# A third expert's tokens turned by DMA instead of TensorE, and two router counts handed out one slot later

## The chip, the cores and the metric

The kernel runs on one core of a Trainium2 chip. The metric is the device time of one execution in microseconds (us), as a median of several runs; a lower time is better. Engines are named as the profile does: PE is TensorE (PEld its weight loads), DVE is VectorE, ACT is ScalarE, POOL is GpSimd, SP is the engine that issues most DMAs.

## The reference, cut to what matters

A windowed attention over 8 batches and 8 heads gives 4608 tokens of 512 values. A mixture of 8 experts follows. Every expert takes exactly 576 tokens, given out greedily in the order of the largest logits:

```python
cap = N // E                       # 4608 // 8 = 576
logits = x @ w_gate
order = np.argsort(-logits.flatten())
for idx in order:                  # the best free (token, expert) pair first
    tok, e = int(idx) // E, int(idx) % E
    if assigned[tok] >= 0 or counts[e] >= cap:
        continue
    assigned[tok] = e
    counts[e] += 1
for e in range(E):
    mask = assigned == e
    out[mask] = np.maximum(x[mask] @ w1[e], 0.0) @ w2[e]
```

## The kernel before

The attention runs first and writes its tokens `x` to device memory. The experts follow from about 230 us on. In what order the experts are done is decided on the chip: the *router* finds, in phases 0 to 7, the expert that is full next and the list of its 576 tokens. Below, "expert k" is the k-th that is worked on (k = 0 to 7), and phase k of the router gives its number (`r.ei[k]`) and its token list (`r.idx[k]`).

**An expert** has two layers. `layer1` (lines 1077 to 1107) makes 8 blocks f of 128 hidden values for 576 tokens, cut in two halves of 288. Each value is held as a high and a low part in a reduced float32 format (`xh` and `xl` for tokens, two planes of a weight tile), and three products are added, so a block has 24 matmuls, the layer 192. ACT evicts a result with Relu (line 1100), and DVE makes its low part (line 1105); four PSUM banks serve for this. `layer2` (lines 1109 to 1137) makes five output tiles t of 128 tokens (the last one of 64) from 24, the last one 16, matmuls, 112 in all, in two PSUM banks; ACT evicts (line 1130), and POOL scatters the rows to the output (line 1135).

**Weights** come in chunks: SP loads one (line 994), ACT casts the high part (line 1001), DVE subtracts for the low part (line 1003, two per chunk).

**Tokens** of expert k + 1 are brought while expert k is worked on. POOL gathers five tiles of token rows by an indirect DMA (line 1012). They must be turned, so that the 512 values lie along the partitions. There are two ways:

- `turn` (lines 1023 to 1042): per tile four transposes on PE (line 1036), ACT rounds the result into `xh` (line 1039), DVE subtracts for `xl` (line 1040).
- `turn_by_dma` (lines 1047 to 1075): per tile two copies on ACT split the 32-bit words into two planes of 16 bits (line 1056), SP issues a transposing DMA (line 1061), two copies on ACT put the words together again (line 1071), ACT rounds into `xh` (line 1073), DVE subtracts for `xl` (line 1074).

`BY_DMA = 2` says that the second way is taken while experts 2 to 6 are worked on, so for the tokens of experts 3 to 7. The tokens of experts 0, 1 and 2 go the first way.

**Slots.** `layer1` yields 16 times and `layer2` 15 times; at each yield `slot(k, i)` (lines 1219 to 1256) hands out side work, with i from 0 to 30. In layer 1 a slot is 12 matmuls long. In layer 2 a tile has three slots, of 9, 9 and 6 matmuls (of 6, 6 and 4 in the last tile). Due slots are written in tables: `W_LOAD` and `W_SPLIT` for the weights of this and the next expert, `DMA_AT[k]` for the 16 steps of `turn_by_dma` (gather, five pairs of plane copies, five transposes, five times word copies with rounding and subtraction). The first way starts at slot 16 with the gather, three slots later with the first tile, and goes on with every second slot.

The router's phases are one generator. What it yields is the number of slots until it goes on: in `few` (lines 886 to 936) a phase makes a comparison of candidates on DVE (`ind`, line 617), yields `WAITS[2]` = 3 slots plus `FAR` = 2 in the first of three steps of phases 1 to 3, and then counts with eight small matmuls on PE (line 641). One slot after that comes a sum over the partitions (line 661), three slots later the next count; after the third step follow line 796 (one slot), lines 822 and 823 (three slots) and the token list from line 853 (four slots). A phase may go on only while the list for expert k + 1 or k + 2 is still missing.

**What sets the order on an engine.** A slot says when an instruction is handed out, and so its rank. A builder then fills each engine's queue before the run: it works with estimated durations, takes the ready instruction of the highest rank, and can put work earlier or later than its slot. On the chip each queue runs in that order, and a waiting instruction holds up what stands behind it. `behind` (line 1044) keeps plane and word copies behind the last eviction that was handed out before them. `xh` and `xl` have one buffer each, the ring `g` of token tiles and planes has seven.

Of the kernel before, what the change touches and what calls it, by code (L numbers as in the profile page):

```python
# [445 lines left out]
WAITS = (2, 1, 3, 1, 1, 3, 3)  # L446
TURN_WAIT, TURN_STEP = (6, 3), (1, 2)
TURN0 = 3
BY_DMA = 2
DMA_AT = {2: [10, 11, 11, 12, 12, 12, 13, 13, 13, 13, 13, 23, 24, 25, 26, 27], 3: [0, 4, 5, 6, 7, 8, 9, 9, 9, 9, 9, 18, 20, 22, 24, 26]}  # L450
BEHIND = mybir.DependencyInfo(mybir.DependencyClass.NoSync, mybir.DependencyReason.SCHED_ONLY)
BIG = 1e30
MAGIC = 12582912.0
# [1 line left out]
CUTS = 2  # L455
STEPS = 3
FEW = 16
FAR = 2
FIRST = 27
EARLY_CUTS = 3  # L460
EXACT_STEPS = 12
# [3 lines left out]
def bc(ap, shape):  # L465
    return ap.to_broadcast(shape)
# [17 lines left out]
class Router:  # L484
# [401 lines left out]
    def few(self, k, b, am, sel):  # L886


        nc, rt = self.nc, self.p["rt"]
        lo, w, rw = yield from self.ends(b, False)  # L890
        q, t = self.small("q", NT), self.small("qt", NT)
        nc.vector.tensor_scalar(w, w, 1.0 / J ** 2, None, ALU.mult)
        nc.vector.tensor_scalar(rw, rw, float(J ** 2), None, ALU.mult)
        half = self.small("half")
        nc.vector.scalar_tensor_tensor(half, w, 0.5, lo, ALU.mult, ALU.add)
        nc.vector.tensor_scalar(q, b, self.hi[:, 0:1], half[:, 0:1], ALU.min, ALU.max)
        nc.vector.tensor_scalar(q, q, half[:, 0:1], rw[:, 0:1], ALU.subtract, ALU.mult)
        nc.vector.tensor_scalar(q, q, MAGIC, MAGIC, ALU.add, ALU.subtract)
        nc.vector.scalar_tensor_tensor(t, q, 8.0, am, ALU.mult, ALU.add)
        nc.vector.scalar_tensor_tensor(t, b, BIG, t, ALU.is_lt, ALU.mult)  # L900
        c = self.small("few", FEW)
        for i in range(0, FEW, 8):
            nc.vector.max(c[:, i:i + 8], t)
            if i + 8 < FEW:
                nc.vector.match_replace(t, c[:, i:i + 8], t, 0.0)
        f, y = self.small("fq", FEW), self.small("fy", FEW)
        nc.vector.tensor_scalar(y, c, 0.125, -0.5625, ALU.mult, ALU.add)
        nc.vector.tensor_scalar(f, y, MAGIC, MAGIC, ALU.add, ALU.subtract)
        fa = rt.tile([128, FEW], BF, name="fa")
        nc.vector.scalar_tensor_tensor(fa, f, -8.0, c, ALU.mult, ALU.add)  # L910
        OH = rt.tile([128, 8, FEW], BF, name="OHf")
        nc.vector.tensor_tensor(OH, self.C["eb"][:, :, 0:FEW], bc(fa.unsqueeze(1), [128, 8, FEW]), ALU.is_equal)
        base = None
        for s in range(STEPS):
            step = float(J ** (2 - s))
            if s == 0:
                nc.vector.tensor_scalar(y, f, 1.0 / step, -0.5 + 0.5 / step, ALU.mult, ALU.add)
            else:
                nc.vector.tensor_scalar(y, f, base[:, 0:1], 1.0 / step, ALU.subtract, ALU.mult)
                nc.vector.tensor_scalar(y, y, float(J), -0.5 + 0.5 / step, ALU.min, ALU.add)  # L920
            key = rt.tile([128, FEW, 2], BF, name="kf")
            nc.vector.tensor_scalar(key, bc(y.unsqueeze(2), [128, FEW, 2]), MAGIC, MAGIC, ALU.add, ALU.subtract)
            ind = rt.tile([128, NT, J], BF, name="ind", bufs=1)
            self.indicate(ind, key, 0, FEW)
            yield WAITS[2] + (s == 0 and k < 4) * FAR
            cnt = self.count(ind, OH, 0, FEW)
            n = yield from self.enough(cnt, self.base)
            low = self.small("lq")
            if s == 0:
                nc.vector.memset(low, -step)  # L930
            else:
                nc.vector.tensor_scalar(low, base, -step, None, ALU.add)
            base = self.small("bq")
            nc.vector.scalar_tensor_tensor(base, n[:, 0:1], step, low, ALU.mult, ALU.add)
        nc.vector.tensor_scalar(sel, q, base[:, 0:1], None, ALU.is_ge)
        nc.vector.scalar_tensor_tensor(self.hi, base, w[:, 0:1], lo, ALU.mult, ALU.add)
# [252 lines left out]
def layer_moe(tc, P, C, r, x, w1, w2, out, exact):  # L1189
# [29 lines left out]
    def slot(k, i):  # L1219
# [18 lines left out]
        for e, layer, c, due in W_SPLIT:  # L1238
            e += k
            if i >= due and len(W.get((e, layer), (0,) * 9)) == c and len(raws[e, layer]) > c:  # L1240
                W[e, layer].append(m.split(raws[e, layer][c]))
                break
        if k >= BY_DMA and k + 1 in r.idx:
            if k not in gathers:
                asked[k + 1] = []
                gathers[k], st["made"] = m.turn_by_dma(r.idx[k + 1], asked[k + 1]), 0
            due = DMA_AT[min(k, 3)]
            while st["made"] < len(due) and i >= due[st["made"]]:
# [108 lines left out]
```

## Time and profile before

| | us |
|---|---|
| median of 3 runs | 678.37 (676.81 to 679.53) |
| the profiled execution, its own time | 674.45 |
| its span, first to last instruction | 672.7 |
| TensorE busy in it | 646.4 |
| VectorE busy | 471.6 |
| ScalarE busy | 384.0 |
| expert 1, layer 2 (from 319.07) | 30.37 |
| expert 2, layer 1 (from 349.44) | 28.81 |
| expert 2, layer 2 (from 378.25) | 27.07 |

The page gives busy times of the engines and shares of the chain that ended last. The views in order of time give the start of each instruction in us from the start of the span, its duration, and in brackets the idle time of its engine before it with what ended it. Neighbours of one kind are merged (x2 and so on). The time of a stretch is read from starts: a matmul's end is modelled, and one begins before the one ahead of it has ended.

### The profile page before, as it was taken

How to read it: one execution, taken by the hardware profiler on the slowest of the kernel's cores; microseconds unless marked ns; L12 is line 12 of the kernel's file. 1: busy time of each engine (PE TensorE's matmuls, PEld its weight loads, DVE VectorE, ACT ScalarE, POOL GpSimd, SP SyncE). 2: the span in 40 equal slices, each digit the busy share in tenths (PEclk: the TensorE clock that was granted, in tenths of full speed). 3: DMA queues.
4: the chain of work that ended last, by engine and by line, in shares of the span. 5: the costliest groups of instructions: out<-in, count | busy, mean ns of one | idle time of the engine just before them, and what ended most of it. 6: DMA issues, size and time to landing. Idle time of an engine off the chain costs nothing.

```text
span 672.7 us, 18974 instructions
## 1 busy us (share of the span) xinstructions
PE 646.4 (96%) x7152; PEld 573.0 (85%) x7152; DVE 471.6 (70%) x1985; ACT 384.0 (57%) x1096; POOL 136.2 (20%) x296
## 2 busy tenths in 40 slices
PE   8999999999995799999999999999999999999996
PEld 5999998888984498889779879989989989988985
DVE  6898888888986899879669788866756625423310
ACT  7998988789973253334234566465545555654200
POOL 4121122122120301511423123023014014011011
PEclk9999999999997799999999999999999999999999
DMA  8656756556521543615406637527536556421001
GB/s 291 191 188 198 222 183 204 185 167 208 163 78 54 155 166 118 235 40 188 165 34 236 171 103 240 118 106 219 117 111 213 132 119 201 128 71 40 1 25 51
DMA packets 58980, 98.13 MB, mean 146 GB/s; under 512 B 27648, under 2 KB 37120, under 8 KB 58880
## 3 DMA queue, kind: packets, MB, share of 16 engines
q1 hardware_dynamic: 52992, 77.96, 38.5%
q0 software_dynamic: 5888, 18.88, 8.5%
q8 instruction: 58, 0.95, 0.6%
q14 instruction: 42, 0.34, 0.2%
HBM read 72.04 MB, written 18.87 MB: 135 GB/s over the span
## 4 chain that ended last, share of the span: by engine, by line
PE 78%; DVE 13%; DMA 3%; ACT 2%; issue 2%; POOL 0%; SPq 0%; POOLq 0%; DVEq 0%; ACTq 0%
PE ph L1095 22%; PE po L1123 9%; PE po L1124 9%; PE s L66 7%; PE po L1126 7%; PE pt L66 7%; PE pt L178 6%; PE x L66 6%; DVE hl L1003 3%; DMA raw<-in_w_dram 2%; DVE hlo L1105 2%; ACT u L159 2%; PE m L641 1%; DMA g<-x,idx 1%; PE pg L1036 1%
## 5 line engine op out<-in xcount | busy, mean ns | idle before, releaser
L1095 PE MATMUL ph<-xh,hl 128*128 128x288 f32 (+2 forms) x1024 | 188.5, 298 | 0.4 <-DVE hlo L1105 0.3
L1095 PEld LDWEIGHTS ph<-xh,hl 128*128 128x128 f32 x1024 | 154.7, 189 | 2.0 <-issue 0.8
L1123 PE MATMUL po<-hl,hh 128*128 128x512 f32 (+1 forms) x328 | 128.4, 391 | 0.0
L159 ACT ACTIVATE u<-u,mn 128x192 f32<-128x192 f32 (+2 forms) x288 | 125.4, 439 | 2.9 <-DVE mn L149 2.9
L1124 PE MATMUL po<-hl,hh 128*128 128x512 f32 (+1 forms) x328 | 126.3, 385 | 0.0
L1095 PE MATMUL ph<-xl,hl 128*128 128x288 f32 (+2 forms) x512 | 115.6, 297 | 0.0
L1100 ACT ACTIVATE hh<-ph 128x288 fp32r<-128x288 f32 (+2 forms) x128 | 46.6, 408 | 106.4 <-PE ph L1095 103.4
L1126 PE MATMUL po<-hl,hlo 128*128 128x512 f32 (+1 forms) x264 | 101.3, 384 | 0.0
L1003 DVE TENSOR_TENSOR hl<-raw,hl 128x512 fp32r<-128x512 f32 x128 | 85.2, 684 | 22.8 <-ACT hl L1001 22.6
L149 DVE CUSTOM_DVE_ANT_0 u<-s,bm 128x192 f32<-128x192 f32 (+2 forms) x308 | 91.9, 333 | 8.1 <-PE s L66 4.5
L1135 POOL DMA_INDIRECT out_dram<-o,idx x40 | 41.8, 1045 | 273.6 <-ACT o L1130 206.4
L1095 PEld LDWEIGHTS ph<-xl,hl 128*128 128x128 f32 x512 | 84.2, 189 | 0.2 <-DVE xl L1074 0.2
L1001 ACT CAST hl<-raw 128x1024 fp32r<-128x1024 f32 x64 | 65.8, 1050 | 23.9 <-DMA raw<-in_w_dram 21.4
L1105 DVE SCALAR_TENSOR_TENSOR hlo<-ph,hh 128x288 fp32r<-128x288 f32 (+2 forms) x128 | 49.2, 416 | 32.2 <-ACT hh L1100 31.5
L1123 PEld LDWEIGHTS po<-hl,hh 128*128 128x128 f32 x328 | 61.8, 188 | 11.2
L1124 PEld LDWEIGHTS po<-hl,hh 128*128 128x128 f32 x328 | 61.7, 188 | 11.2
L1130 ACT COPY o<-po 128x512 f32<-128x512 f32 (+1 forms) x33 | 18.9, 574 | 90.1 <-PE po L1126 79.9
L66 PE MATMUL s<-qk 64*64 64x192 f32 (+1 forms) x1112 | 62.4, 320 | 2.2 <-issue 1.1
L178 PE MATMUL pt<-ident_sb,u 128*128 128x128 f32 x368 | 57.7, 278 | 0.7 <-ACT u L159 0.6
L1126 PEld LDWEIGHTS po<-hl,hlo 128*128 128x128 f32 x264 | 49.6, 188 | 9.9
L1012 POOL DMA_INDIRECT g<-x,idx x40 | 43.0, 1075 | 64.9 <-DMA raw<-in_w_dram 26.5
L159 ACT ACTIVATION_READ_ACCUMULATOR u<-u,mn 128x1 f32 x288 | 55.2, 192 | 0.0
(249 smaller groups left out, 921.2 us busy)
## 6 DMA issues: line engine op xcount, KB each, us to landing
raw<-in_w_dram SPq DMA_DIRECT2D x64, 512.0 KB, 4.4
qk<-in_qk_dram SPq DMA_DIRECT2D x32, 576.0 KB, 4.5
v<-in_v_dram SPq DMA_DIRECT2D x32, 288.0 KB, 3.0
x<-xb SPq DMA_DIRECT2D x14, 512.0 KB, 3.5
x<-xb SPq DMA_DIRECT2D x8, 128.0 KB, 3.3
x<-xb SPq DMA_DIRECT2D x4, 256.0 KB, 2.2
g<-x,idx POOLq DMA_INDIRECT x40, 4.2
out_dram<-o,idx POOLq DMA_INDIRECT x40, 2.8
```

Of the source, the lines that this page charges most:

```text
L66: put(nc.tensor.matmul(out, w, a, start=start, stop=stop, skip_group_check=True))
L149: put(nc.vector.tensor_tensor_reduce(out=u[rows], in0=x[rows, c:c + 64 * m].rearrange("q (j k) -> q j k", k=64), in1=bm[n % NP][rows, y:y ...
L159: put(nc.scalar.activation(u, u, AF.Exp, bias=st["mn"][:, i:i + 1], scale=-1.0, accum_out=st["sm"][:, i:i + 1]))
L178: put(nc.tensor.transpose(ps[:, c:c + 128], u[:, o + 128 * j:o + 128 * j + 128], ident))
L1001: self.last = nc.scalar.copy(hl[:, 0, :], raw)
L1003: nc.vector.tensor_tensor(hl[:, 1, c:c + 512], raw[:, c:c + 512], hl[:, 0, c:c + 512].bitcast(F32), ALU.subtract)
L1095: nc.tensor.matmul(pp[t], w[:, a, j, fo:fo + 128], x[:, j, cut[t]:cut[t + 1]], start=(i == 0), stop=(i == 11))
L1100: self.acted = nc.scalar.activation(o, pp[t], AF.Relu)
L1105: nc.vector.scalar_tensor_tensor(d, pp[t][:, c0:c1], 0.0, o[:, c0:c1].bitcast(F32), ALU.max, ALU.subtract)
L1123: nc.tensor.matmul(out, a, wh, start=(f == 0), stop=False)
L1124: nc.tensor.matmul(out, a, wl, start=False, stop=(f == 7 and t == 4))
L1126: nc.tensor.matmul(out, hl[:, f, 128 * t:128 * t + 128], wh, start=False, stop=(f == 7))
```

## The change

Two things change. `BY_DMA` becomes 1, so the tokens of expert 2 are turned in the second way, while expert 1 is worked on. A row of due slots is added for it: the gather at slot 14, the plane copies at 15 and 16, the transposes at 17, word copies, roundings and subtractions at 23 to 27. And `FAR` becomes a table by phase: it stays 2 for phases 1 and 2, becomes 3 for phase 3 (it was 2) and 1 for phase 4 (it was 0).

```diff
-BY_DMA = 2
-DMA_AT = {2: [10, 11, 11, 12, 12, 12, 13, 13, 13, 13, 13, 23, 24, 25, 26, 27], 3: [0, 4, 5, 6, 7, 8, 9, 9, 9, 9, 9, 18, 20, 22, 24, 26]}
+BY_DMA = 1
+DMA_AT = {1: [14, 15, 15, 16, 16, 16, 17, 17, 17, 17, 17, 23, 24, 25, 26, 27], 2: [10, 11, 11, 12, 12, 12, 13, 13, 13, 13, 13, 23, 24, 25, 26, 27], 3: [0, 4, 5, 6, 7, 8, 9, 9, 9, 9, 9, 18, 20, 22, 24, 26]}
...
-FAR = 2
+FAR = (0, 2, 2, 3, 1, 0, 0, 0)
...
-            yield WAITS[2] + (s == 0 and k < 4) * FAR
+            yield WAITS[2] + (FAR[k] if s == 0 else 0)
```

## Rows read from the trace of the kernel before

**Rows 1.** The page: busy time, share of the span and instructions of each engine; the chain that ended last by engine.

```profile
PE 646.4 (96%) x7152; PEld 573.0 (85%) x7152; DVE 471.6 (70%) x1985; ACT 384.0 (57%) x1096; POOL 136.2 (20%) x296
...
PE 78%; DVE 13%; DMA 3%; ACT 2%; issue 2%; POOL 0%; SPq 0%; POOLq 0%; DVEq 0%; ACTq 0%
```

**Rows 2.** Busy time by engine in three layers: expert 1's layer 2, expert 2's layer 1 and layer 2 (stretch, its length, then busy us and instructions of PE, PEld, DVE, ACT and POOL, the granted clock of TensorE as a share of full speed, the DMA share and GB/s); and the one line of a late layer 1 from the chain in order of time (start, length, matmuls).

```profile
319.07:349.44 30.37, 29.54 (x162) 23.25 (x161) 18.14 (x69) 8.71 (x14) 10.31 (x9) 1.00 0.31 109
349.44:378.25 28.81, 27.71 (x230) 26.77 (x229) 27.12 (x108) 14.64 (x29) 7.47 (x8) 1.00 0.61 199
378.25:405.32 27.07, 27.07 (x146) 21.37 (x144) 21.75 (x98) 14.38 (x25) 4.69 (x5) 1.00 0.43 116
...
564.34 25.58 PE ph L1095 x192
```

**Rows 3.** The transposes in expert 1's layer 2: the line's matmuls in that stretch, then TensorE in order of time at the second and at the last of the five groups.

```profile
L1036 PE MATMUL pg<-ident_sb,g x20: 222/272/307, 327.8 to 345.2; 128*128 128x128 f32 x16, 64*128 64x64 f32 x4
...
331.87 0.60 PE L1036 MATMUL pg<-ident_sb,g 128*128 128x128 f32 x4
332.22 0.47 PE L1123 MATMUL po<-hl,hh 128*128 128x512 f32 x1
332.54 0.39 PE L1124 MATMUL po<-hl,hh 128*128 128x512 f32 x1
...
344.97 0.46 PE L1036 MATMUL pg<-ident_sb,g 64*128 64x64 f32 x4
345.36 0.50 PE L1123 MATMUL po<-hl,hh 128*128 128x512 f32 x1
```

**Rows 4.** TensorE in order of time around the first count of phase 3, and VectorE's comparison for that count.

```profile
326.12 0.39 PE L1124 MATMUL po<-hl,hh 128*128 128x512 f32 x1
326.35 0.39 PE L1126 MATMUL po<-hl,hlo 128*128 128x512 f32 x1
327.56 0.42 PE L641 MATMUL m<-OHf,ind 128*128 128x16 bf16 x8 [0.83 <-DVE ind L617]
...
326.81 0.69 DVE L617 TENSOR_TENSOR ind<-kf,c_i 128x1024 bf16<-128x1024 bf16 x1
```

**Rows 5.** TensorE around the first count of phase 4 in expert 2's layer 1, VectorE's comparison for it, the matmuls of layer 1 alone up to phase 3's token list (line 853) and up to that count (stretch, length, PE busy and matmuls, PEld), and the engines' busy time from phase 3's last sum to the comparison's end.

```profile
372.85 0.69 PE L1095 MATMUL ph<-xh,hl 128*128 128x288 f32 x4
374.37 0.42 PE L641 MATMUL m<-OHf,ind 128*128 128x16 bf16 x8 [0.83 <-DVE ind L617]
...
373.62 0.69 DVE L617 TENSOR_TENSOR ind<-kf,c_i 128x1024 bf16<-128x1024 bf16 x1
...
349.44:359.55 10.11, 9.78 (x72) 9.53 (x71) 1.00 0.56 197
349.44:374.36 24.92, 23.46 (x170) 22.63 (x169) 1.00 0.64 215
...
347.09:374.32 27.23, 26.18 (x201) 24.93 (x200) 26.61 (x101) 12.85 (x24) 8.19 (x9) 1.00 0.61 206
```

**Rows 6.** The way by DMA as it runs for expert 3's tokens: groups of instructions with their busy time and mean ns (plane copies over the whole span, word copies and roundings in expert 2's layer 2), the five issues on SP, and the end of it in order of time on ScalarE, VectorE and TensorE.

```profile
L1056 ACT COPY pl<-g 128x512 uint16<-128x512 uint16 x40 | 22.2, 627 | 1.1 <-DMA g<-x,idx 1.1
...
L1071 ACT COPY xf<-tp 128x512 uint16<-128x512 uint16 x8 | 5.6, 778 | 0.0
...
L1073 ACT CAST xh<-xf 128x512 fp32r<-128x512 f32 x4 | 2.5, 620 | 0.1
...
L1061 SPq DMA_TRANSPOSE tp<-pl x5: 1231/1261/1358, 376.1 to 382.9; - x5
...
403.19 0.41 ACT L1073 CAST xh<-xf 128x256 fp32r<-128x256 f32 x1
403.50 2.00 ACT L1001 CAST hl<-raw 128x1024 fp32r<-128x1024 f32 x2
...
405.36 0.42 DVE L1074 TENSOR_TENSOR xl<-xf,xh 128x256 fp32r<-128x256 f32 x1
...
405.58 0.66 PE L1095 MATMUL ph<-xl,hl 128*128 128x288 f32 x2
406.08 0.29 PE L1095 MATMUL ph<-xh,hl 128*128 128x288 f32 x1
```

**Rows 7.** Around the gather for expert 2: VectorE's token list, GpSimd's first and last gather with the time from issue to landing, the weight loads on SP, the eviction of layer 2's first tile and the late weight casts on ScalarE; and from the page the low halves of the weights.

```profile
316.72 0.33 DVE L861 SCALAR_TENSOR_TENSOR idx<-ia 64x5 int32<-64x5 f32 x2
...
317.83 1.22 POOL L1012 DMA_INDIRECT g<-x,idx  x1 [12.54 <-issue]
...
323.40 2.52 POOL L1012 DMA_INDIRECT g<-x,idx  x1 [0.30 <-issue]
...
DMA to landing us min/median/max: 3.5/5.5/6.5
...
319.81 1.66 SPq L994 DMA_DIRECT2D raw<-in_w_dram  x2
...
324.78 0.59 ACT L1130 COPY o<-po 128x512 f32<-128x512 f32 x1 [4.00 <-PE po L1126]
...
346.59 2.11 ACT L1001 CAST hl<-raw 128x1024 fp32r<-128x1024 f32 x2 [0.75 <-PE po L1124]
...
L1003 DVE TENSOR_TENSOR hl<-raw,hl 128x512 fp32r<-128x512 f32 x128 | 85.2, 684 | 22.8 <-ACT hl L1001 22.6
```

## The prediction

> **What bounds the kernel now.** I read the first two parts of the page, then the busy time by layer of the experts, then the instructions in order of time around each place that the diff touches. TensorE is busy 96% of the span and carries 78% of the chain that ended last [rows 1]; its granted clock is 1.00, the higher of its two levels (2.4 GHz), in the layers in question [rows 2]. So a microsecond is won only where TensorE issues less or waits less. In the experts it hardly waits at all: PE is idle for 0.83 us in expert 1's layer 2, for 1.10 us in expert 2's layer 1, and not at all in expert 2's layer 2 [rows 2]. The two layers with waits are the ones that the diff touches. Layer 2 of expert 1 (30.37 us) also carries the transposes of expert 2's tokens; layer 2 of expert 2 (27.07 us), beside which the next tokens go by DMA, does not.
>
> A busy share hides part of a wait, since the end of a matmul is modelled. I therefore count from start to start: a layer 2 matmul starts every 0.23 us [rows 4], a layer 1 matmul every 0.133 us (a late layer, without router work, has 192 in 25.58 us, [rows 2]).
>
> **Part 1: expert 2's transposes leave TensorE.** Twenty transposes in five groups of four stood in expert 1's layer 2 [rows 3]. A group that follows the router's count costs 0.39 us up to the next matmul (344.97 to 345.36); there are three such. A group alone costs 0.35 us (331.87 to 332.22), and the matmul behind it lasts 0.32 instead of 0.23 us until the next start, which makes 0.44 us; there are two. Sum: 3 x 0.39 + 2 x 0.44 = 2.05 us, all of it on the bounding engine. The count's own switch stays.
>
> **Part 2: what replaces them.** Ten plane copies on ScalarE of 0.63 us each, ten word copies (eight of 0.78, the two short ones taken no dearer), five roundings of 0.62 [rows 6]: at most 6.3 + 7.8 + 3.1 = 17.2 us, less the five evictions that go. ScalarE is busy only 8.71 of 30.37 us in that layer [rows 2], so the sum fits. VectorE's five subtractions change their input, not their number. The gather is handed out at slot 14 instead of 16, but that moves nothing: GpSimd starts it at 317.83, right after the index is written at 316.72 + 0.33 [rows 7]. SP gets five transposes of about 1.3 us [rows 6]. The loads that could queue behind them, two chunks of expert 2's first weights, are issued from 319.81 on, before any plane can exist (first landing 317.83 + 3.5 = 321.3), and their casts start at 346.59 [rows 7]: 25 us of cover, so nothing.
>
> What isn't hidden is the end. The last part of the tokens goes word copy, rounding, subtraction, and layer 1 begins at once. For expert 3, which already goes this way, the last rounding ran 403.19 to 403.60 and its subtraction 405.36 to 405.78, while layer 1 asks for it at 405.58; the two matmuls from there take 0.50 us to the next, where 2 x 0.133 are due, a loss of about 0.25 us [rows 6]. Expert 2's will follow the same slots 23 to 27. Bounds: 0, not below, since expert 2's layer 1 starts without such a gap now, and the 4.8 us of the last rival below; I take 0.25, from the nearest row.
>
> Taken by itself the new way is the slower one: four transposes pass TensorE in 0.35 to 0.39 us [rows 3], one transposing DMA keeps SP for about 1.3 us [rows 6]. I go by who is the bound: TensorE is, SP isn't. A rule of the Trainium skill speaks against this part: "VectorE: DVE Perf Modes", The three transpose paths and Rules for kernel authors, gives a 128x128 transpose (of 16-bit values) 390 ns on TensorE and 1309 ns by the DMA crossbar, and advises TensorE wherever a PSUM destination will do. The trace agrees on the order of the two; by the rule the time would rise, and the last rival works out by rows what that would be, 680.4.
>
> **Part 3: phase 3's first count one slot later.** In expert 1's layer 2 the matmul after 326.35 was due at 326.58 and started at 327.56: 0.98 us of wait for the comparison that VectorE ran 326.81 to 327.50 [rows 4]. It stood at its due slot 19: 326.58 is 7.51 us, or some 33 matmuls of 0.23, behind the layer's start, the 24 of the first tile and nine of the second. Slot 20 lies nine matmuls, 9 x 0.23 = 2.07 us, further, more than the 0.98 that is missing, and the comparison does not wait for the count, so it would be 1.1 us early. Gain 0.98 us; bounds 0 and 0.98.
>
> **Part 4: phase 4's first count.** The same wait stands in expert 2's layer 1: due at 372.85 + 4 x 0.133 = 373.38, started at 374.37, 0.99 us, behind the comparison at 373.62 [rows 5]. But here the due time isn't what places it. Phase 3's last step stood after 72 matmuls, slot 5; two slots and three later is slot 10, 132 matmuls; the count stands after 170 [rows 5]. The built order has already put it back to where the comparison was thought ready, and VectorE is busy 26.61 of the 27.23 us up to there [rows 5]. Phase 3's extra slot makes phase 4's due slot 12 (6 + 2 + 4), 156 matmuls, still ahead of 170. So the extra slot of phase 4 need not bind, and VectorE's chain, which starts about a slot later as well, sets the time. Bounds: 0.99 gained, and 1.6 lost if the whole slot (12 x 0.133) shows; I take 0, since the row that decides is VectorE's busy one.
>
> The rest of phases 3 and 4 moves by one and two slots. Expert 3's gather waits for phase 3's index, so its planes come up to 1.6 us later; between the planes' transposes (slot 13) and their use (slot 23) lie ten slots, which hide it. If that cover were gone, TensorE would pay it one to one. Phase 5 is held back until expert 3 in both, so nothing moves behind it.
>
> **Sum.** -2.05 - 0.98 + 0.25 = -2.78 us. The profiled execution took 674.45 us, 672.7 of span and 1.75 around it; 671.7 would be its time afterwards. The median of the runs shown lies 3.92 us above that execution, at 678.37; the saving is a count of matmuls and waits and doesn't scale with that, so 675.6.
>
> **Rivals.**
> A second wait that goes too: the slot binds after all, or VectorE's order changes in favour. -2.78 - 0.99 = -3.77, 674.6. For it: the first wait has the same size and cause. Against it: 170 against 132.
>
> ScalarE's queue blocked: the plane copies wait for the gather, and the eviction of layer 2's first tile (324.78) stands behind them. The last gather is issued at 323.40 and lands at most 6.5 us after its issue [rows 7], 329.9; two copies and the eviction (0.59) end near 331.7. The third tile, which needs the bank, would start near 332.22 - 0.98 - 0.39 - 0.35 = 330.5. Loss up to 1.2, so 676.8. For it: one gather wait of 1.1 us stands before the plane copies already [rows 6]. Against it: in order of readiness the eviction comes first.
>
> The other side, late tokens: the two weight casts that become possible at 346.59 (2.11 us, [rows 7]) go ahead of the last word copies on ScalarE, and their four low halves (4 x 0.68, [rows 7]) ahead of the last subtraction on VectorE. For expert 3 the casts came behind the last rounding, but directly, at 403.50 [rows 6]. Layer 1 of expert 2 then starts 2.1 + 2.7 = 4.8 us late: -2.78 + 4.8 = +2.0, 680.4. It decides against the change from a lateness of 2.8 us on top of the 0.25. This is what the transpose rule quoted above would amount to: a longer path that nothing hides any more.
>
> **How the numbers follow.** Chances: forecast 0.42, second wait gone too 0.25, blocked eviction 0.18, late tokens 0.15. The range goes from the second case less the 1.2 us by which the runs shown spread, 673.4, to the last case, 680.4. About 0.5% (3.4 us) is what a measurement of this kernel can tell from no change: below 675.0 or above 681.8. The forecast lies 0.6 us inside "same", so with a spread of 1.2 to 1.6 us it gives about 0.13 to faster, the second case 0.16, the third 0.02: 0.31. Slower gets part of the last case and a little for what isn't listed, 0.10; the rest, 0.59, is same.
>
> **What would show it.** Right: no transposes of line 1036 in layer 2 of expert 1, that layer near 27.3 us; no wait of TensorE for the comparison in it; a wait of about 1 us still in layer 1 of expert 2; two or three stretched starts when that layer begins. Wrong: a gap ahead of layer 2's third tile (blocked eviction), a gap of over 1 us at expert 2's first matmuls (late tokens), a count in expert 2 that starts without a wait, or new gaps in experts 2 and 3 from planes that come late.

## The result, and the profile after

The changed kernel takes 680.75 us (median of 20 runs, 677.71 to 684.99), the kernel before 677.49 (20 runs, 675.34 to 680.05): a ratio of 1.0053 with a 95% interval of 1.0037 to 1.0068, by the ratio some 3.6 us slower. The forecast was 2.8 us faster, 675.6, and the dearest of its rivals 680.4. The profiled execution took 681.35 us, 679.6 of it span. That of before was faster than each of the 20, so two more profiles of the kernel before and one more of the changed kernel were taken. Lengths from start to start, in us:

| stretch | before, three profiles | after, two profiles |
|---|---|---|
| time of the execution | 674.45, 679.38, 680.10 | 681.35, 683.15 |
| expert 1, layer 2 | 30.37, 30.46, 30.44 | 33.75, 34.17 |
| expert 2, layer 1 | 28.81, 30.97, 29.84 | 28.48, 29.58 |
| expert 2, layer 2 | 27.07, 27.06, 27.04 | 28.81, 29.60 |
| expert 3, layer 1 | 27.60, 28.61, 28.88 | 28.88, 28.74 |

The loss is in expert 1's layer 2, where the gain had been forecast: 3.5 us, by the means of the profiles. Expert 2's layer 2 adds 2.2; the two layers 1 differ about as much between executions of one kernel.

The page, busy time by engine (answers to [rows 1]): TensorE has its twenty instructions less, ScalarE its twenty more.

```profile
PE 645.5 (95%) x7132; PEld 572.5 (84%) x7132; DVE 470.6 (69%) x1985; ACT 395.6 (58%) x1116; POOL 135.7 (20%) x296
```

Busy time in three layers (answers to [rows 2], same columns), then in two stretches of the first of them.

```profile
318.07:351.82 33.75, 29.32 (x142) 23.00 (x140) 17.12 (x66) 19.58 (x34) 8.17 (x8) 0.90 0.49 134
351.82:380.30 28.48, 27.54 (x224) 26.60 (x223) 26.93 (x109) 12.73 (x25) 8.65 (x9) 1.00 0.61 195
380.30:409.11 28.81, 27.53 (x153) 21.53 (x152) 20.09 (x83) 16.79 (x30) 4.99 (x4) 1.00 0.42 109
...
329.13:333.99 4.86, 0.43 (x3) 0.05 (x2) 1.77 (x6) 3.33 (x6) 1.01 (x1) 0.78 0.63 128
333.99:338.40 4.41, 4.41 (x11) 3.45 (x12) 1.48 (x6) 0.11 (x1) 0.98 (x1) 0.50 0.94 187
```

PE is idle for 4.4 of 33.75 us where it was idle for 0.83, and the granted clock is 0.90 where it was 1.00. Both come from one place. TensorE in order of time around phase 3's first count (answers to [rows 4]):

```profile
327.39 0.39 PE L1126 MATMUL po<-hl,hlo 128*128 128x512 f32 x1
327.62 0.42 PE L641 MATMUL m<-OHf,ind 128*128 128x16 bf16 x8
...
329.12 0.40 PE L1126 MATMUL po<-hl,hlo 128*128 128x512 f32 x1
333.94 0.19 PE L661 MATMUL m<-sat,c_ones 128*128 128x1 bf16 x1 [4.43 <-DVE sat L658]
333.99 0.78 PE L1123 MATMUL po<-hl,hh 128*128 128x512 f32 x1
334.56 0.63 PE L1124 MATMUL po<-hl,hh 128*128 128x512 f32 x1
334.99 0.63 PE L1126 MATMUL po<-hl,hlo 128*128 128x512 f32 x1
```

The count itself (327.62) starts without a wait, as forecast. Behind a count VectorE works out the router's answer to it (lines 649 to 658), and a sum on TensorE takes that answer. This sum starts 4.82 us after the matmul ahead of it, where 0.23 are due: 4.6 lost. Behind it eleven matmuls take 4.41 us instead of 11 x 0.23 = 2.5, at a granted clock of 0.50 (the 1.2 GHz level): 1.9 more. Who was late is to be read in the chain that ended last, in order of time (start, length, what):

```profile
321.14 7.03 DMA g<-x,idx
328.19 0.28 ACT pl L1056
...
328.90 1.65 ACT pl L1056 x3
330.55 0.48 ACT o L1130
331.03 0.95 ACT hl L1001
332.01 1.29 DVE hl L1003 x2
...
333.74 0.16 DVE sat L658
333.94 0.19 PE m L661
```

The chain is: a gather's landing, plane copies, an eviction, a weight cast, its two low halves on VectorE, the answer, TensorE. Of these, only the plane copies need the gather. The two queues in order of time, first ScalarE's, then VectorE's:

```profile
318.13 0.71 ACT L1100 ACTIVATE hh<-ph 128x288 fp32r<-128x288 f32 x2 [1.00 <-PE ph L1095]
320.59 1.14 ACT L1056 COPY pl<-g 128x512 uint16<-128x512 uint16 x2 [1.74 <-DMA g<-x,idx]
323.57 1.14 ACT L1056 COPY pl<-g 128x512 uint16<-128x512 uint16 x2 [1.84 <-DMA g<-x,idx]
327.33 3.22 ACT L1056 COPY pl<-g 128x512 uint16<-128x512 uint16 x6 [2.62 <-issue]
330.46 0.57 ACT L1130 COPY o<-po 128x512 f32<-128x512 f32 x1
330.94 1.04 ACT L1001 CAST hl<-raw 128x1024 fp32r<-128x1024 f32 x1
```

```profile
324.82 0.69 DVE L617 TENSOR_TENSOR ind<-kf,c_i 128x1024 bf16<-128x1024 bf16 x1
332.01 1.29 DVE L1003 TENSOR_TENSOR hl<-raw,hl 128x512 fp32r<-128x512 f32 x2 [6.50 <-ACT hl L1001]
333.34 0.17 DVE L649 TENSOR_TENSOR odd<-m,base 64x8 f32<-64x8 f32 x1
```

In the kernel before, ScalarE's order of time reads at this place:

```profile
319.13 0.71 ACT L1100 ACTIVATE hh<-ph 128x288 fp32r<-128x288 f32 x2 [0.90 <-PE ph L1095]
319.73 1.05 ACT L1001 CAST hl<-raw 128x1024 fp32r<-128x1024 f32 x1
```

The cast ran directly behind the activations, 0.7 us into the layer; now ten plane copies stand between, with three waits of 1.74 to 2.62 us among them, and it runs 12.9 us into the layer. VectorE does nothing for 6.50 us; the router's answer was possible when the count was done, near 328, and stands behind the low halves. The second profile shows the same wait, 4.77 us from start to start.

Phase 4's first count (answers to [rows 5]) still waits: it was due at 376.33 + 2 x 0.133 = 376.60 and starts 0.84 us later.

```profile
376.33 0.42 PE L1095 MATMUL ph<-xh,hl 128*128 128x288 f32 x2
377.44 0.42 PE L641 MATMUL m<-OHf,ind 128*128 128x16 bf16 x8 [0.68 <-DVE ind L617]
```

Expert 2's layer 2 has a smaller case of the same kind: expert 3's last planes wait for their gather at 380.17, casts follow at 381.81 and 383.34, their low halves stand between the router's comparison and its answer, and the sum (386.21) starts 1.66 us after the matmul ahead of it (2.44 in the second profile).

### The profile page after: what moved, and what is told of

Same layout as the page of the kernel before. It is cut to its first block, busy times and chain, and to the rows that moved or that the text cites. A ratio compares the mean times of both kernels' runs of the same rounds, so it can differ in the third digit from the quotient of the medians.

```text
span 679.6 us, 18963 instructions
## 1 busy us (share of the span) xinstructions
PE 645.5 (95%) x7132; PEld 572.5 (84%) x7132; DVE 470.6 (69%) x1985; ACT 395.6 (58%) x1116; POOL 135.7 (20%) x296
## 4 chain that ended last, share of the span: by engine, by line
PE 77%; DVE 8%; DMA 5%; ACT 5%; issue 4%; POOL 1%; SPq 0%; POOLq 0%; ACTq 0%
PE ph L1095 23%; PE po L1123 9%; PE po L1124 9%; PE s L66 7%; PE pt L66 7%; PE po L1126 7%; PE pt L178 6%; PE x L66 6%; DMA g<-x,idx 2%; DVE hl L1003 2%; DMA raw<-in_w_dram 2%; ACT u L159 2%; ACT hl L1001 1%; ACT xf L1071 1%; DVE hlo L1105 1%
## 5 line engine op out<-in xcount | busy, mean ns | idle before, releaser
L1012 POOL DMA_INDIRECT g<-x,idx x40 | 41.2, 1031 | 67.3 <-DMA raw<-in_w_dram 26.8
```

## Experiments

Theory 1: the plane copies wait in ScalarE's queue, what stands behind them comes late, and by way of VectorE's queue the router's answers. Rival 1: the router's later slots cost the time. Rival 2: the way by DMA is too long for expert 2 in any order. Ratios are to the kernel before on the same chip, with 95% intervals.

**The two parts alone.**

```diff
-FAR = (0, 2, 2, 3, 1, 0, 0, 0)
+FAR = (0, 2, 2, 2, 0, 0, 0, 0)      # turn_only
-BY_DMA = 1
+BY_DMA = 2                          # far_only
```

> Only the tokens' way is changed (expert 2 by DMA as planes); the router's first counts keep their old slots. Theory 1 (ScalarE's queue: ten plane copies wait for the gather, a weight cast and the first eviction stand behind them, the cast's low halves on VectorE stand ahead of the router's answer, and TensorE waits for that answer): the plane copies still stand ahead of the cast, so layer 2 of expert 1 keeps a gap of over 3 us and is still above 32 us (33.74 with the whole change), and the kernel stays 2 to 4 us slower than before. Rival 1 (the later slots of the router cost the time): with the old slots the layer falls below 30 us and the kernel is 1 to 3 us faster than before.

> Only the router's first counts are later (phases 3 and 4); expert 2's tokens go through TensorE as before. Theory 1: no plane copies in layer 2 of expert 1, so no gap behind the count; the first wait of 0.98 us goes, the second stays, the kernel is 0 to 1 us faster than before. Rival 1 (the later slots cost the time): layers of experts 2 and 3 grow as with the whole change (layer 2 of expert 2 27.07 to 28.82, layer 1 of expert 3 27.60 to 28.88 us), and the kernel is 2 to 4 us slower than before.

The tokens alone: 1.0065 (1.0043 to 1.0088), 4.4 us slower, layer 2 of expert 1 at 35.70 us. That layer (columns as above), and TensorE's waits in it (us in total, times, longest):

```profile
318.07:353.77 35.70, 29.68 (x142) 22.96 (x141) 18.05 (x69) 19.81 (x34) 9.01 (x9) 0.90 0.46 126
...
PE m L661 <- DVE sat L658: 6.0, 2, 5.8
```

The later slots alone: 1.0021 (1.0005 to 1.0036), 1.4 us slower; layer 2 of expert 1 gains 1.1 us (29.33). So the tokens' way costs the larger part without the slots, as theory 1 has it, and the slots a smaller part, as rival 1 has it; theory 1 had expected the slots alone to gain up to 1 us. The two don't add: with both it is 3.6 us, less than 4.4 + 1.4.

**The later slots, one by one.**

```diff
+FAR = (0, 2, 2, 3, 0, 0, 0, 0)      # far3, with BY_DMA = 2
+FAR = (0, 2, 2, 2, 1, 0, 0, 0)      # far4, with BY_DMA = 2
```

> Tokens as before; only phase 3's first count is one slot later, phase 4's stays. If the 1.4 us that the later slots cost come from phase 4's slot: layer 2 of expert 1 falls by 1.0 us (as with both slots, 29.33), layer 1 of expert 2 stays at 28.5 to 29.3, and the kernel is 0.5 to 1 us faster than before. If they come from phase 3's: layer 1 of expert 2 is at 31 us as with both, and the kernel is 1 to 1.5 us slower than before.

> Tokens as before; only phase 4's first count is one slot later. If phase 4's slot costs the 1.4 us: layer 1 of expert 2 above 30 us, layer 1 of expert 3 near 29, the kernel 1 to 2.5 us slower than before. By the prediction's part 4 (the slot doesn't bind, the count moves by four matmuls only): no difference over 0.5 us.

1.0037 (1.0018 to 1.0057) and 1.0035 (1.0016 to 1.0053): each is slower, neither less so than the two together, as far as the intervals tell. far3 has the 1.05 us in layer 2 of expert 1 (29.32) and gives it back; far4 has not (30.35). In both a sum in layer 1 of expert 3 starts 2.48 us after the matmul ahead of it, and that layer takes 30.20 and 31.72 us. To know what of this is the spread of executions, second and third profiles were taken:

> The kernel before once more, for a second profile of it. The first was taken of an execution at 674.45 us, under the lowest of the timed ones. If its waits in layer 1 of expert 2 (1.13 us ahead of the count) and layer 1 of expert 3 (0.38 us at the answer) are typical, they return within 0.3 us; if they belong to that fast execution, they are 1.7 and up to 2.5 us, as in the kernels with later slots, and the cost of the later slots is smaller than the difference of the profiles.

> The kernel before, a third profile. Layer 1 of expert 2 was 28.81 and 30.97, layer 1 of expert 3 27.60 and 28.61 in the first two. Values in this range say that the spread of these two layers alone, about 3 us, makes the spread of the kernel's time (674.5 to 681.5).

> The later slots alone, a second profile. Layer 2 of expert 1 at 29.3 again (1.0 less than before). If the later slots make the next layers longer in each execution, layer 1 of expert 2 is over 31 and layer 1 of expert 3 about 29 again; if that is the spread of executions, layer 1 of expert 2 lies anywhere from 28.5 to 31.5.

> The changed kernel once more, for a second profile. The gap of 4.8 us at the first answer in layer 2 of expert 1 and the stretch at half clock behind it are there again within 1 us if they come from the order of the queues; if they were an accident of one execution, the layer is below 31 us.

Layers of the later slots alone, second profile (expert 1's layer 2 to expert 3's layer 1), then a stretch in the second of them:

```profile
318.48:347.81 29.33, 29.33 (x162) 23.16 (x160) 17.44 (x67) 8.72 (x14) 9.60 (x8) 1.00 0.33 113
347.81:380.20 32.39, 30.17 (x224) 28.92 (x222) 28.14 (x112) 15.08 (x30) 8.18 (x9) 0.91 0.62 187
380.20:408.10 27.90, 27.90 (x152) 21.92 (x152) 18.51 (x78) 14.34 (x25) 4.98 (x4) 0.98 0.32 94
408.10:437.10 29.00, 27.80 (x222) 26.53 (x221) 24.88 (x99) 14.52 (x29) 6.91 (x6) 1.00 0.66 188
...
374.80:379.90 5.10, 5.10 (x28) 4.95 (x29) 3.35 (x14) 3.71 (x7) 0.00 (x0) 0.50 0.50 102
```

Layer 1 of expert 2 is 31.40 and 32.39 us with the later slots, 28.81 to 30.97 without; layer 2 27.38 and 27.90 against 27.04 to 27.07. The count of phase 4 waits 1.9 us from start to start in both profiles (1.1 to 1.7 in the three of before), and a stretch at clock 0.50 follows. But one profile of before has such a stretch too, in the same layer:

```profile
376.90:380.00 3.10, 3.10 (x15) 2.95 (x15) 2.02 (x11) 3.10 (x7) 0.00 (x0) 0.50 0.30 62
```

So the half clock is part of the spread of this kernel's time; far3's profile, with a count that waits 1.9 us in the same layer, doesn't have it. In the means of these profiles the later slots win 1.1 us in expert 1's layer 2 and lose 2.0, 0.6 and 0.6 in the three layers behind it, 2.1 in sum; the timed runs say 1.4. far3 and far4 alone lose in another place: layer 1 of expert 2 (30.28 and 29.54) lies within the spread of before, layer 1 of expert 3 (30.20 and 31.72) above it. The sum that starts there 2.48 us after the matmul ahead of it does so after 0.38, 1.36 and 1.60 us in the three profiles of before; what delays it further stays open.

**The order in ScalarE's queue.**

```diff
-DMA_AT = {1: [14, 15, 15, 16, 16, 16, 17, 17, 17, 17, 17, 23, 24, 25, 26, 27], ...
+DMA_AT = {1: [14, 18, 18, 18, 18, 18, 20, 20, 20, 20, 20, 23, 24, 25, 26, 27], ...   # planes_late
```

The table hands out the planes two to three slots later and the transposes three; the text below says four for the planes.

> The whole change, with expert 2's ten plane copies four slots later in the planner's list, so that the weight cast and the first eviction of layer 2 come ahead of them in ScalarE's queue. Theory 1: the wait of 4.8 us behind the count goes, and the stretch at half clock behind it with it; layer 2 of expert 1 takes 27 to 28 us instead of 33.74, and the kernel is 5 to 6.5 us faster than with the whole change, 2 to 3 us faster than before. Rival 1 (later slots): nothing of the router is moved, the time stays within 1 us of the whole change. Rival 2 (the way by DMA is too long for expert 2 in any order): planes that come later make expert 2's first matmuls wait, so what layer 2 of expert 1 gains layer 1 of expert 2 loses, over 31 us instead of 28.48.

1.0011 (0.9996 to 1.0026), 0.4% less than the whole change. The cast runs at 318.43, the eviction at 323.45, the planes behind both, and the first wait is gone. But the layer takes 32.42 us; VectorE and TensorE near its end, in order of time:

```profile
341.88 0.69 DVE L1074 TENSOR_TENSOR xl<-xf,xh 128x512 fp32r<-128x512 f32 x1 [4.01 <-ACT xh L1073]
...
342.70 0.69 DVE L617 TENSOR_TENSOR ind<-kf,c_i 128x1024 bf16<-128x1024 bf16 x1
```

```profile
341.67 0.39 PE L1124 MATMUL po<-hl,hh 128*128 128x512 f32 x1
343.45 0.42 PE L641 MATMUL m<-OHf,ind 128*128 128x16 bf16 x8 [1.39 <-DVE ind L617]
...
344.94 0.40 PE L1124 MATMUL po<-hl,hh 128*128 128x512 f32 x1
348.17 0.19 PE L661 MATMUL m<-sat,c_ones 128*128 128x1 bf16 x1 [2.83 <-DVE sat L658]
```

The end of the way by DMA does what its start had done: the first subtraction of expert 2's tokens waits 4.01 us for a rounding, phase 3's last comparison stands behind it, and the last answer behind a later one. This is theory 1's kind of cause, at a place that it had not named, and its forecast for this run (2 to 3 us faster than before) was missed. Two runs move one more thing each:

```diff
+DMA_AT = {1: [14, 18, 18, 18, 18, 18, 20, 20, 20, 20, 20, 27, 27, 27, 27, 27], ...   # xl_last
+DMA_AT = {1: [14, 18, 18, 18, 18, 18, 20, 20, 20, 20, 20, 23, 24, 25, 26, 27], ...   # late_old
+FAR = (0, 2, 2, 2, 0, 0, 0, 0)                                                       # late_old
```

> The plane copies four slots later, as in the run that undid the first block, and besides the word copies, roundings and subtractions of expert 2's tokens in the last slot, behind the router's third count. Theory 1 with the short window: no answer of the router waits in layer 2 of expert 1 any more, which ends near 345 (27.3 to 29 us), and the lateness stands open where it belongs, as a wait at expert 2's first matmuls: the transposes end near 340 and 10.7 us of copies follow, so tokens are ready near 350 and layer 1 of expert 2 takes 4 to 7 us more (32 to 36). Sum of the two layers 60 to 64 us, as in the other orders (59.2 before, 60.95 with the planes four slots later, 62.2 with the whole change). If instead the order on VectorE is the whole cost and the way is short enough, the sum is 56 to 57 and the kernel 2 us or more faster than before.

> Expert 2's tokens by DMA with the plane copies four slots later, and the router's first counts in their old slots. If the later slots cost 0.21% in this order too, the kernel is 0.1% faster than before (676 to 678.5 where before is 677.5; with the later slots it was 0.11% slower). If the old slot brings the count back behind the plane copies and the first wait, layer 2 of expert 1 is above 33 us and the kernel 0.3% or more slower.

xl_last: 1.0041 (1.0023 to 1.0059). No answer waits behind a subtraction in layer 2 of expert 1 (29.55 us), and expert 2's first matmuls wait instead (31.37 for the layer):

```profile
346.55 0.28 PE L796 MATMUL m<-T,c_ones 128*128 128x288 bf16 x1 [0.36 <-DVE T L793]
348.66 0.61 PE L1095 MATMUL ph<-xh,hl 128*128 128x288 f32 x1 [1.83 <-ACT xh L1073]
```

late_old: **0.9965 (0.9949 to 0.9981)**, 2.4 us faster than before. Layers as above:

```profile
319.15:348.81 29.66, 27.43 (x142) 21.30 (x141) 16.54 (x67) 18.43 (x34) 10.02 (x9) 1.00 0.54 152
348.81:377.38 28.57, 27.13 (x222) 26.41 (x221) 26.84 (x107) 14.62 (x30) 7.47 (x8) 1.00 0.60 197
```

With phase 3 one slot earlier its last comparison runs at 338.49, ahead of the first subtraction (340.94). Two waits are left (1.21 us from start to start at the first count, 1.81 at the last answer), no half clock follows, and expert 2 begins without a gap. Rival 2 falls: the way is tight, but one order of it fits. The later slots cost 0.46% in this order (1.0011 with them, 0.9965 without) and 0.21% alone; the intervals don't tell these two apart.

The cleanest pair for theory 1 is late_old and turn_only: their tables differ by the slots of the planes and the transposes alone. Layer 2 of expert 1 takes 29.66 us instead of 35.70, the kernel 0.9965 of before instead of 1.0065. And the early planes had bought nothing, as SP's transposes show, first in the changed kernel, then in late_old:

```profile
329.58 8.81 SPq L1061 DMA_TRANSPOSE tp<-pl  x5
...
330.21 8.41 SPq L1061 DMA_TRANSPOSE tp<-pl  x5
```

The first planes are ready at 321.7 in the changed kernel and at 326.5 in late_old, and the first transpose starts near 330 in both, 0.07 us after the copies of the fourth tile (until 329.51 and 330.14). A likely reason, which no run tested, is the ring `g`: five gathers and two pairs of planes fill its seven buffers, so the first transpose gets the buffer of the fourth tile, and has to wait until it has been copied.

**The victim.**

```diff
             W[e, layer].append(m.split(raws[e, layer][c]))
+            if (k, e, layer, c) == (2, 2, 1, 1): m.behind(m.last)       # cast_later
```

> The whole change, but the one weight cast that stood behind the plane copies (second chunk of expert 2's layer 2 weights) is not pulled into layer 2 of expert 1; the plane copies still stand ahead of the layer's first eviction. This tells the victim. If it is the cast, by way of its low halves on VectorE: the 4.8 us behind the count and the half clock go, layer 2 of expert 1 takes 27.3 to 28.5 us (with up to 1.2 us for the third tile's bank, by the prediction's blocked eviction), the kernel is 4 to 6 us faster than with the whole change. If it is the eviction and its PSUM bank: the gap stays at over 3 us, only its releaser changes, and the time stays within 1.5 us of the whole change.

1.0105 (1.0081 to 1.0129), slower than the whole change, though the wait at the first answer is gone. TensorE's waits in layer 2 of expert 1 (32.56 us):

```profile
PE m L661 <- DVE sat L658: 2.1, 1, 2.1
PE po L1123 <- ACT o L1130: 1.5, 1, 1.5
```

The second is the PSUM bank of the prediction's blocked eviction; its price there was up to 1.2. The first is an answer behind a subtraction again. The edit moved more than one cast: the next two, at 349.11 and 350.36 in the changed kernel, come with it, at 361.08 and later. The layers behind are long (30.96, 29.47 and 30.27 us up to the end of expert 3's layer 1); that the late casts make them so is not shown. So the cast was the victim in the changed kernel and the eviction the next in line; both expectations were too simple.

**Plane copies on GpSimd, for expert 2 only.**

```diff
-                self.behind(nc.scalar.copy(pl[:r, a, :], words[:r, :, 1 - a]))
+                nc.gpsimd.tensor_copy(pl[:r, a, :], words[:r, :, 1 - a])
```

> The whole change, with expert 2's plane copies on GpSimd instead of ScalarE, so that nothing in ScalarE's queue waits for the gather. If ScalarE's queue alone were the cause: layer 2 of expert 1 27 to 28.5 us, the kernel 5 to 6 us faster than with the whole change. By theory 1 with the short window: the wait of 4.8 us behind the first count goes, but the word copies still end near 348 us and VectorE's subtractions hold up the router's next counts, as with the planes four slots later (there 1.4 + 2.8 us of waits), so the layer takes 31 to 33 us and the kernel is within 1.5 us of that run's 678.4.

1.0046 (1.0030 to 1.0062), and no clean test of the order: in the time of the ten copies on GpSimd two small operations of VectorE, 0.18 us each in the changed kernel, take 1.66 and 3.85 us (VectorE, then GpSimd).

```profile
326.17 1.66 DVE L908 TENSOR_SCALAR fq<-fy 128x16 f32<-128x16 f32 x1
327.86 3.85 DVE L910 SCALAR_TENSOR_TENSOR fa<-fq,few 128x16 bf16<-128x16 f32 x1
```

```profile
326.07 5.61 POOL L1057 COPY pl<-g 128x512 uint16<-128x512 uint16 x10
```

The comparison comes late by that, and TensorE waits 3.9 us for it. The Trainium skill, "SBUF — State Buffer", SBUF: two separate sides, says that VectorE, in a two-port mode or with two inputs in SBUF, and GpSimd share one pair of ports, which the one that starts first holds for its whole instruction while the other stands still. The rows agree that VectorE stands still, but for longer than one instruction of GpSimd: at 0.56 us a copy, the second operation lasted for some seven copies.

**What the transposes cost, and a token list that is early.** In no_turn expert 2's transposes, evictions, roundings and subtractions are left out of the kernel before; in early_index, which builds on turn_only, the gather takes expert 1's index from slot 4 on.

```diff
+                gathers[k], st["turn"] = m.turn(gs) if k != 1 else iter(()), ...              # no_turn
+                gathers[k], st["made"] = m.turn_by_dma(r.idx[k + (k != 1)], asked[k + 1]), 0   # early_index
```

> The kernel before without the twenty transposes, five evictions, roundings and subtractions of expert 2's tokens; the gather stays, and expert 2 computes on the tokens left over from expert 1 (its outputs are left wrong). This measures part 1 by itself, the most that moving the turn off TensorE can give: 2.05 us by the prediction, so layer 2 of expert 1 at 28.0 to 28.6 us instead of 30.37 and the kernel 1.8 to 3 us faster than before. If the transposes had been hidden, under 0.7 us.

> Only the tokens' way is changed (router's slots as before), and expert 2's gather takes expert 1's index, which is ready a whole layer earlier, so that the gather and the planes can begin in layer 1 of expert 1. This kernel computes expert 2's outputs from expert 1's tokens; the work is the same in size. Theory 1, as the first four runs leave it (the way gather, planes, transposes, word copies needs about 33 us from the index on, layer 2 of expert 1 offers 27, and the in-order queues of ScalarE and VectorE hand the lateness on to the router's answers): with the early index nothing is late, layer 2 of expert 1 takes 27.5 to 28.5 us instead of 35.70, and the kernel is 1.5 to 3 us faster than before, the gain that the prediction's parts 1 and 2 gave. Rival 2 (the DMA way costs the time in itself, by its copies on ScalarE or its transposes on SP): the layer stays above 31 us and the kernel 2 us or more slower than before.

no_turn: 0.9955 (0.9938 to 0.9971), 3.1 us faster, layer 2 of expert 1 28.15:

```profile
318.34:346.49 28.15, 27.25 (x143) 21.30 (x141) 14.96 (x64) 6.20 (x9) 8.90 (x9) 1.00 0.32 118
```

early_index: 1.0113 (1.0088 to 1.0138), and it tells nothing of theory 1 against rival 2. The early gathers went out right behind expert 1's, in layer 2 of expert 0, which takes 34.76 instead of 28.75 us, and the transposes still began at 329.91, since on SP they stand behind the weight loads.

## Why the prediction was wrong

**Part 1 was right.** The transposes cost 2.3 us in the layer (28.15 against 30.42, the mean of three) where 2.05 were forecast, and 3.1 in the kernel with an interval of 2.0 to 4.2. As no_turn leaves out their evictions, roundings and subtractions too, this is the most that they cost.

**Part 2 failed.** The step is the sum of ScalarE's work: "ScalarE is busy only 8.71 of 30.37 us in that layer [rows 2], so the sum fits." It fits by busy time (19.58 of 33.75 after). What counts is where the copies stand. Each engine's queue runs in order, ten copies that wait for a gather stand ahead of work that waits for nothing, and 4.6 + 1.9 us come of it: with the 27.3 us that the prediction gave the layer this makes 33.8, and 33.75 were measured. The cost that the part did take, 0.25 us for a late end of the tokens, was read off expert 3, whose planes are copied from 370.58 on for use at 405.6, 35 us; expert 2's first planes, at 320.59, have 25 us until the layer's end without waits (318.07 + 27.3). That this is a matter of order, not of sums, is shown: with the later slots, later planes took 0.4% off; with the old slots they took 1.0% off, and left the kernel 0.35% faster than before, 0.1% from leaving the turn out.

**The blocked eviction was half of it.** This rival had the mechanism, and "Against it: in order of readiness the eviction comes first" was the wrong step: the built order put the planes first. It had the wrong victim, and so the wrong price. It looked for who waits for ScalarE on TensorE alone, and found a bank at 1.2 us (1.5 when the cast was out of the way). The way that decided goes through a second queue, ScalarE to VectorE to TensorE. The prediction named two late weight casts with 25 us of cover and called them expert 2's first weights; they are second-layer weights, and another chunk of these, the cast at 319.73, which the builder pulls ahead of its slot, went unseen.

**Part 3 was right where it looked.** The wait of phase 3's first count is gone in each kernel with the later slot but planes_pool, where the comparison itself was held up; and without other changes layer 2 of expert 1 gets 1.1 us shorter (0.98 forecast).

**Part 4 and the rest, taken at nothing, were mis-sized.** With the later slots alone layer 1 of expert 2 is about 2 us longer, its layer 2 0.6; the kernel loses 1.4 us (0.3 to 2.4) instead of the forecast 0.98 gain. "VectorE's chain, which starts about a slot later as well" was seen, but the bound of 1.6 us falls short of the 2.0 measured in that layer; the half clock behind a longer wait was in no bound. In the order of planes_late the slot also puts phase 3's last comparison behind a subtraction. Expert 3's planes, said to be hidden by ten slots, came late enough in the changed kernel to hold up casts and an answer (the 2.2 us of expert 2's layer 2). That layer takes 27.02 in turn_only, 27.38 and 27.90 with the slots alone, and 27.38 in planes_late, which has both parts; why the gather lands late in the changed kernel stays open.

**The late tokens** did not come in the changed kernel, whose waits gave the tokens time; they came in xl_last, where the price was 1.8 us of wait and a stretch of half clock, not 4.8. The rule of the Trainium skill that the prediction weighed ("VectorE: DVE Perf Modes", Rules for kernel authors: TensorE for a transpose wherever a PSUM destination will do) gives the right sign for the kernel as changed; late_old, by DMA too and faster than before, shows that the price of one transpose does not decide here.

## What to carry to other kernels

Before work that waits for a DMA is put on an engine, write down what stands behind it in that engine's queue, and who waits for each of these on the next engine, to the second step: a free engine share says nothing about it. Put such work behind what is ready, and keep the short answers that the bounding engine waits for ahead of it. Ask also what an early start buys: here the next step waited for one of the last gathers in any order. And take two or three profiles of the kernel before: here one layer repeats within 0.1 us and the next differs by 2, and one profile doesn't tell which is which.

## What was not expected of the hardware

After some waits TensorE runs at a granted clock of 0.50 (matmuls of 512 columns start every 0.43 us instead of 0.23, those of 288 every 0.24 instead of 0.13). It followed waits of 6.2 us (turn_only), 4.8 (the changed kernel), 4.3 (planes_pool) and 3.2 (planes_late), counted from start to start. Of two waits of 2.48 us only the one in far4 was followed by it, not the one in far3; of the waits of 1.9 us ahead of phase 4's count the two with the later slots were, and the one in far3 was not; of two waits of 1.72 us in the kernel before, the one in the second profile was, and the one in the third was not. So the length of the wait alone doesn't decide. The half clock costs about half of its length: 1.9 us in the changed kernel, by the same share some 1.5 (of 3.10) in the second profile of the kernel before and some 2.5 (of 5.10) with the later slots. A wait on the bounding engine can so cost more than the time that it lasts: 40% more in the changed kernel (1.9 on the 4.6 lost), more than twice as much in the second profile with the later slots (2.5 on the 1.8 lost).
